# One written list for batch 0 behind its attention: tails, weight pieces, attention blocks and products taken singly

## The chip, the cores and the metric

The kernel runs on one core of a Trainium2 chip. A core has a matrix engine (PE), a vector engine (DVE), a scalar engine (ACT), a general engine (POOL) and SP, which here only issues DMAs. Each engine works through its own instructions in the order in which the program wrote them, and waits at semaphores for the others. The metric is the device time of one execution in microseconds (us), taken as the median over runs. Before the change it was 1199.24 us in three runs (1198.79 to 1200.69).

## The reference

Attention with a sigmoid in the place of the softmax, for 8 batches of 12 heads (448 tokens, 64 dimensions a head), then two dense layers with a gate of their own:

```python
scores = scale * np.matmul(q, k.transpose(0, 1, 3, 2)) - np.log(S)
attn = 1.0 / (1.0 + np.exp(-scores))
attn_out = np.matmul(attn, v).astype(np.float32)
...
h = x @ w_in          # x: 3584 x 768, w_in: 768 x 2048
g = h - np.tanh(h)
return (g @ w_out).astype(np.float32)
```

## The kernel before

**Arithmetic.** fp32 numbers are mostly multiplied as three fp16 products: a high and a low half of each factor, without low times low. The weights come as 64-bit patterns. Each has to be converted to fp32 on the chip (a "piece" is 128 rows of one part of a matrix: load, sign, bits, and a small matmul `wl` that sums magnitudes for a bound), and later split in place into its fp16 halves: `high` on ACT (a few on DVE), `low` on DVE. The slot of a high half is where the fp32 numbers of an earlier row block lay, so a split of one row block waits for those before it.

**Stages of batch 0.** `attention32` computes the attention of batch 0 in fp32 while `w_in` is converted. Then the first dense layer of batch 0 runs in fp32 (`ph` matmuls on unsplit weights, 16 of them in eight pairs, as the hidden units come in 16 groups of 128). After each pair comes its tail (`mix`): ACT makes a square `u` and a tanh `th` from the PSUM tile `ph`, DVE makes `m` and `th` from the same tile, two more squares and products follow, and `halves` writes the fp16 halves `g` of the pair. Only when DVE has read `ph` for `m` and `th` is that PSUM buffer free. Then the second layer (`moe2`) multiplies `g` by the split `w_out`: for batch 0 the left half of the columns first (e = 0: three full token tiles, each of eight products of six matmuls), then the right half (e = 1), then 16 short products for the last 64 tokens.

**What runs beside it.** Batch 0 also has to carry three other streams: the conversion of `w_out` (20 pieces while the first layer runs, 12 more beside the second), the in-place split of `w_out` and `w_in`, and the attention of batch 1 with the first block of batch 2. The attention stream is the generator `stream`. Its first eight steps are preparation (loads, norms, scales, the fp16 halves of K and Q); from step 9 on they are blocks of scores (`sc` on PE), sigmoid (`a` on ACT) and the product with v (`acc` on PE). Each block takes the two PSUM buffers of tag `sc` in turn, and the `ph` pairs use the same two.

**What sets the order.** For the first layer the function `moe1_32` does: after each `ph` group a fixed number of conversion steps (`REST`), at some groups one step of the attention stream (`INIT`), and after each pair its whole tail in one go. The tail of the eighth pair is taken in four portions in `first`, between attention blocks 9 to 13. From then on `second` works off a table of due times (`SPLIT`, `CONV`, `BLOCKS0`, counted in products): after each product everything that is due is written. The order of PE, ACT, DVE and POOL is that of the program there; the DMA issues on SP are placed by the framework. Batches 1 to 7 have tables of their own (`BLOCKS1`, `BLOCKS`).

Of the kernel before, what the change touches and what calls it, by code (L numbers as in the profile page):

```python
# [8 lines left out]
F16 = mybir.dt.float16  # L9
BF16 = mybir.dt.bfloat16  # L10
F32 = mybir.dt.float32
# [22 lines left out]
class Builder:  # L34

    AV32 = 2

    INIT = (0, 4, 6, 7, 8, 10, 12, 14)
    EARLY = 4
    AHEAD = 3  # L40
    LAND = ("o", "o", 2, "v", "v", "v", 1, 0, 3, 4, 5)
    REST = (4, 4) + (2, 1, 1) * 4 + (1, 0)
    SPLIT = tuple(8 + 1.25 * k for k in range(8)) + tuple(22 + 0.85 * k for k in range(36))
    CONV = tuple(3 + 1.2 * k for k in range(1, 6)) + tuple(9 + 0.85 * k for k in range(1, 13))

    BLOCKS = (8, 11, 16, 19, 20, 24, 27, 32, 35, 36, 40, 43, 48, 51, 52)
    TAIL = (1, 2, 3, 4, 5)
    ALONE = 11
    BLOCKS0 = (4, 6, 8, 9, 12, 16, 20, 23, 24, 31, 38)
    BLOCKS1 = (4, 7, 8, 11, 13, 16, 19, 20, 24, 27, 32, 35, 36, 40, 43, 48, 51, 52)  # L50

    TP = 8
# [283 lines left out]
    def norm(self, t, out):  # L336

        flat = t.rearrange("p a d -> p (a d)") if len(t.shape) == 3 else t
        n = flat.shape[1]
        junk = self.sm.tile([P, 8 * D], BF16, name="sqn", tag="sq", bufs=4)  # L340
        self.nc.scalar.activation(junk[:, :n], flat, AF.Square, accum_out=out)  # L341
# [304 lines left out]
    def attention32(self, b, weights, rest):  # L646

        nc = self.nc
        S = self.S
        NP = self.NP  # L650
        xs = []
        tags = (("kn", "qn"), ("K", "Q"))
        self.row = []
        loaded = {}

        def load(j):
            loaded[j] = self.load_qk(b, j, tags[j % 2])
            if j < 2:
                next(weights)
            loaded[j].append(self.load_v(b, j, self.att, "vhl", 3))  # L660

        load(0)
        one = self.sm.tile([P, 1], F32, name="one", tag="m")
        nc.scalar.activation(one, self.nls, AF.Sigmoid)
        next(weights)
        load(1)
        next(weights)
        todo = []
        accs = {}

        def open_acc(j):
            accs[j] = self.ps.tile([P, 512], F32, name="acc", tag="mm", bufs=2)

        def av():
            j, c, a = todo.pop(0)
            v = loaded[j][2][:, None]
            if c == QT:
                open_acc(j + 1)
                self.av([accs[j], accs[j + 1]], v, a, c, 0)
            else:  # L680
                if c == 0 and j % 2 == 0:
                    open_acc(j)
                self.av([accs[j]], v, a, c, j % 2)
            if c == (QT, QT - 1)[j % 2]:
                xs.append(self.evac_x(j, accs.pop(j), None))

        self.warm(12)
        order = [(j, c) for j in range(NP) for c in (range(QT) if j % 2 else range(QT + 1))]
        for n in range(0, len(order), 2):
            group = order[n : n + 2]  # L690
            pss = []
            for j, c in group:
                both = (j, j + 1) if c == QT else (j,)
                K, Q = ([loaded[i][x][:, None] for i in both] for x in range(2))
                pss.append(self.scores(K, Q, c))
            ready = len(todo)
            todo += [(j, c, self.weigh(ps, 1.0 / math.sqrt(D))) for (j, c), ps in zip(group, pss)]
            if n < 4:
                self.warm(4)
            for _ in range(ready):  # L700
                av()
            for j, c in group:
                if c == 1 and j + 2 < NP:
                    load(j + 2)
                next(weights)
                if c == QT:
                    next(weights)
        next(rest)
        while todo:
            av()  # L710
            next(rest)
        next(rest)
        self.xs, self.xs32 = xs, True

    def token_norms(self, nm):
# [65 lines left out]
    def moe1(self, st):  # L781
# [6 lines left out]
        for k in range(self.NF // 2):  # L788
# [19 lines left out]
                pass  # L808
            if k == 0:
                self.Sg, self.iSg = self.g_scales(m)  # L810

    def moe1_32(self, xs, weights, rest):


        nc = self.nc
        S = self.S
        self.gs = []
        self.late = []
        for k in range(self.NF // 2):
            ph = self.ps.tile([P, 2, 512], F32, name="ph", tag="sc", bufs=2)  # L820
            for e in range(2):
                f = 2 * k + e
                for c in range(self.NC):
                    nc.tensor.matmul(  # L824
                        ph[:, e, :S],
                        self.where("in", c)[:, f * P : (f + 1) * P],
                        xs[c],
                        start=(c == 0),
                        stop=(c == self.NC - 1),
                    )  # L830
                if f in self.INIT:
                    next(self.blocks)
                for _ in range(self.REST[f]):
                    next(rest)
                if k == 0 and e == 0:
                    for _ in weights:
                        pass
                    w = self.w_in_scales()
                    m = self.token_norms(self.ps.tile([P, 512], F32, name="nm0", tag="mm", bufs=2))
                elif k < 2:  # L840
                    next(w, None)
                if (k, e) == (1, 1):
                    self.Sg, self.iSg = self.g_scales(m)
                if f == 12:
                    self.w_out_scale(0)
                    self.ahead = self.split_w_out(0)
                if f > 12:
                    next(self.ahead)
                if f == 15:
                    self.w_out_bound(1)  # L850
                    self.split_in = self.split_w_in()
                    next(self.split_in)
            g = self.gp.tile([P, 2, 2, S], F16, name="g", tag="g")
            self.gs.append(g)
            self.tail = self.mix(ph[:, :, :S], g, self.ih0, self.ihk0)
            if k == self.NF // 2 - 1:
                return
            for _ in self.tail:
                pass

    def mix(self, ps, g, ih, ihk):

# [101 lines left out]
    def build(self):  # L964
# [22 lines left out]
        with tc.manual_schedule(engines={E.PE, E.Activation, E.DVE, E.Pool}):  # L987
# [4 lines left out]
                self.attention32(0, weights, rest)  # L992
            self.gp = tc.alloc_tile_pool(name="gp", bufs=self.NF // 2, reuse_waits="tile")
            self.blocks = self.stream()
            self.moe1_32(self.xs, weights, rest)
            assert next(rest, None) is None
            self.first(self.convert(pieces[nB:], "product"))
        with tc.manual_schedule(engines={E.PE, E.Activation, E.DVE, E.Pool, E.SP}):
            for b in range(1, self.B):
                self.batch(b)  # L1000
        self.gp.release()

    def first(self, rest):

        n = 5
        split, ahead = self.split_in, [self.ahead]
        products = self.moe2(0, self.gs)
        next(self.tail)
        for _ in range(self.AHEAD):
            next(products)  # L1010
        next(split)
        for k in range(n - 1):
            if k == 2:
                next(self.blocks)
            next(self.blocks)
            for _ in range(2):
                next(self.tail, None)
            if k == 1:
                next(ahead[0])
            if k == 2:  # L1020
                self.finish_g()
                next(ahead[0])
        next(rest)
        next(ahead[0])
        next(rest)
        assert n + len(self.BLOCKS0) + len(self.BLOCKS1) == 5 * self.NP + len(self.BLOCKS) - self.ALONE
        assert len(self.SPLIT) == self.NC * self.NB - self.SHIFT
        events = [(p, lambda: next(split)) for p in self.SPLIT]
        events += [(k + 0.5, lambda: next(ahead[0], None)) for k in range(self.AHEAD, self.NF // 2 - 3)]
        events += [(p, lambda: next(rest)) for p in self.CONV]  # L1030
        at = math.ceil(self.CONV[-1])

        def scale():
            self.w_out_scale(1)
            ahead[0] = self.split_w_out(1)

        events += [(at, scale)] + [(at + k, lambda: next(ahead[0], None)) for k in range(1, self.NF // 2 + 1)]
        self.second(0, self.BLOCKS0, len(self.BLOCKS0) - 1, events, products, self.AHEAD)

    def batch(self, b):  # L1040

# [16 lines left out]
            blocks = self.BLOCKS1  # L1058
        self.second(b, blocks, alone, events)

    def second(self, b, blocks, alone, events, products=None, done=0):

        step = lambda: next(self.blocks)
        events += [(p, step) for p in blocks]
        scales = []

        def norms():
            scales.append(self.batch_scales(self.xs, b == 0))
            next(scales[0])

        if blocks:
# [2 lines left out]
            events += [(p, lambda: next(scales[0], None)) for p in (end + 5, end + 7)]  # L1074
        events.sort(key=lambda e: e[0])
        full = self.NF * (self.S // P)
        for k, _ in enumerate(products or self.moe2(b, self.gs), done):
            now = k + 1 if k < full else full + (k + 1 - full) / 2
            while events and events[0][0] <= now:
                events.pop(0)[1]()  # L1080
# [35 lines left out]
```

## Time and profile before

| | before |
|---|---|
| median of the runs | 1199.24 us |
| time of the profiled execution | 1198.76 us |
| its span | 1197.0 us |
| PE busy over the span | 1164.3 us (97%) |
| DVE busy over the span | 904.0 us (76%) |
| ACT busy over the span | 884.0 us (74%) |

The span is the time between the first and the last instruction of the profile; the 1.76 us around it belong to the execution. PE is the engine that bounds the whole, so time can be lost or won where PE waits, or where it runs at less than the full clock. The chain of waits puts 71% of the span on PE and nearly nothing on the other engines. How batch 0 stands out against the rest is shown in the prediction.

### The profile page before, as it was taken

To read this page: it belongs to the slowest core of one execution; us is meant where nothing else is said; L and a number is where in the kernel's file an instruction comes from. 1 tells how busy PE (TensorE), PEld (TensorE's weight loads), DVE (VectorE), ACT (ScalarE), POOL (GpSimd) and SP (SyncE) were. 2 spreads that over 40 slices of the span, in tenths; PEclk is the share of its full clock that TensorE was granted. 3 is DMA by queue.
4 is the path that set the end of the run, shared out by engine and by line. 5 is a ranking of instruction groups with operands and counts; after the bars stand their busy time and mean duration, and the time that the engine had idled before them with its cause. 6 is when DMAs were issued, how large, how long until landed. Compare 5 with 4: busy or idle time off the path is not lost.

```text
span 1197.0 us, 19036 instructions
## 1 busy us (share of the span) xinstructions
PE 1164.3 (97%) x7585; PEld 602.9 (50%) x7585; DVE 904.0 (76%) x1335; ACT 884.0 (74%) x1248; POOL 76.3 (6%) x58
## 2 busy tenths in 40 slices
PE   9999779999999999999999999999999999999998
PEld 2344324455545555555555555555555555555555
DVE  6889868769866897778966798578977699646920
ACT  7878688868988588767788588876887688745820
POOL 0000000000021000200012000110012000200000
PEclk9999899999999999999999999999999999999999
DMA  9941043200122100220022100211012200000000
GB/s 364 344 146 55 16 133 123 67 14 1 39 68 74 38 1 30 82 60 16 1 69 67 52 1 16 74 60 39 1 49 72 67 1 2 29 27 8 1 14 33
DMA packets 34057, 70.43 MB, mean 59 GB/s; under 512 B 3888, under 2 KB 21040, under 8 KB 33968
## 3 DMA queue, kind: packets, MB, share of 16 engines
q1 hardware_dynamic: 33824, 68.99, 17.6%
q8 instruction: 59, 0.97, 0.3%
q14 instruction: 30, 0.25, 0.1%
q10 hardware_dynamic: 144, 0.23, 0.1%
HBM read 58.20 MB, written 11.01 MB: 58 GB/s over the span
## 4 chain that ended last, share of the span: by engine, by line
PE 71%; ACT 1%; DVE 0%; issue 0%; ACTq 0%; DVEq 0%
PE ph L794 27%; PE po L912 27%; PE sc L399 6%; PE acc L430 6%; PE por L950 5%; ACT a L410 0%; DVE ahl L417 0%; PE pbn L349 0%; ACT ahl L416 0%; ACT o L941 0%; PE nm L718 0%; ACT sqn L341 0%; ACT x L444 0%; ACT Q L374 0%; DVE orem L959 0%
## 5 line engine op out<-in xcount | busy, mean ns | idle before, releaser
L912 PE MATMUL po<-wo,g 128*128 128x384 f16 x2304 | 396.8, 327 | 10.1 <-ACT wo L226 4.9
L794 PE MATMUL ph<-xhl,wi 128*128 128x448 f16 x2016 | 382.6, 352 | 0.0
L912 PEld LDWEIGHTS <-g 128*128 128x128 f16 x2304 | 220.2, 98 | 181.1 <-issue 42.9
L794 PEld LDWEIGHTS <-wi 128*128 128x128 f16 x2016 | 196.7, 98 | 185.0 <-issue 2.1
L417 DVE SCALAR_TENSOR_TENSOR ahl<-a,ahl 128x896 f16<-128x896 f32 x126 | 160.8, 1311 | 134.4 <-ACT ahl L416 134.3
L410 ACT ACTIVATE a<-sc,nls,rn 128x896 f32<-128x896 f32 x147 | 156.0, 1091 | 49.1 <-PE sc L399 48.9
L867 ACT ACTIVATE u<-ph,ih 128x896 f32<-128x896 f32 x64 | 64.4, 1006 | 83.8 <-PE ph L794 81.9
L416 ACT ACTIVATE ahl<-a 128x896 f16<-128x896 f32 x126 | 113.2, 941 | 0.6
L399 PE MATMUL sc<-Q,K 64*128 64x448 f16 x1008 | 102.9, 358 | 7.1 <-ACT a L410 6.1
L871 DVE SCALAR_TENSOR_TENSOR m<-ph,ihk,u 128x896 f32<-128x896 f32 x64 | 73.4, 1146 | 37.3 <-ACT th L869 37.0
L778 ACT ACTIVATE g<-m,Sg 128x896 f16<-128x896 f32 x64 | 66.6, 1041 | 33.6 <-DVE m L885 26.2
L885 DVE COPY_PREDICATED m<-u,th 128x896 f32<-128x896 uint32 x64 | 77.3, 1208 | 6.6
L430 PE MATMUL acc<-ahl,vhl 128*64 128x448 f16 (+1 forms) x864 | 80.6, 356 | 0.1
L779 DVE SCALAR_TENSOR_TENSOR g<-m,Sg,g 128x896 f16<-128x896 f32 x64 | 73.2, 1144 | 7.7 <-ACT g L778 7.7
L882 DVE SCALAR_TENSOR_TENSOR m<-q,m 128x896 f32<-128x896 f32 x64 | 69.9, 1092 | 10.2 <-ACT q L881 2.8
L461 POOL TENSOR_TENSOR x<-x 128x448 f32<-128x448 f32 x24 | 26.4, 1098 | 773.2 <-ACT x L444 773.2
L824 PE MATMUL ph<-x,wi 128*128 128x448 f32 x192 | 75.1, 541 | 0.0
L872 DVE SCALAR_TENSOR_TENSOR th<-ph,ih,th 128x896 f32<-128x896 f32 x64 | 73.1, 1143 | 0.0
L884 ACT ACTIVATE u<-u,b 128x896 f32<-128x896 f32 x64 | 66.7, 1043 | 4.0 <-DVE m L871 2.0
L399 PEld LDWEIGHTS <-K 64*128 64x128 f16 x1008 | 36.5, 98 | 65.8 <-issue 41.4
L878 DVE SCALAR_TENSOR_TENSOR m<-q,m 128x896 f32<-128x896 f32 x64 | 69.4, 1084 | 0.0
L950 PE MATMUL por<-wo,g 128*64 128x384 f16 x768 | 65.8, 327 | 1.1 <-ACT o L941 1.1
(139 smaller groups left out, 1144.1 us busy)
## 6 DMA issues: line engine op xcount, KB each, us to landing
knn<-k SPq DMA_DIRECT2D x45, 224.0 KB, 2.6
qnn<-q SPq DMA_DIRECT2D x44, 224.0 KB, 2.6
rawo<-moe_w_out SPq DMA_DIRECT2D x22, 384.0 KB, 5.2
out<-o SPq DMA_DIRECT2D x21, 384.0 KB, 2.3
raw<-moe_w_in SPq DMA_DIRECT2D x13, 512.0 KB, 8.0
vn<-v SPq DMA_DIRECT2D x24, 256.0 KB, 2.9
wo<-moe_w_in SPq DMA_DIRECT2D x11, 512.0 KB, 8.1
vn<-v SPq DMA_DIRECT2D x24, 192.0 KB, 2.4
```

The lines of the kernel that those rows point to most:

```text
L399: self.nc.tensor.matmul(ps[i * m : (i + 1) * m, h, : self.S], K[i][r, w, c * P : c * P + m], Q[i][r, x, :], start=(n == 0), stop=(n == len ...
L410: self.nc.scalar.activation(a[:, 0], ps[:, :, : self.S], AF.Sigmoid, bias=self.nls, scale=scale)
L416: nc.scalar.activation(A[:, 0], a[:, 0], AF.Copy, scale=A_SCALE)
L417: nc.vector.scalar_tensor_tensor(A[:, 1], a[:, 0], A_SCALE, A[:, 0], op0=ALU.mult, op1=ALU.subtract)
L430: self.nc.tensor.matmul(acc[i][h * D : (h + 1) * D, : self.S], v[k, w, 2 * QT + h if half else h * QT + c], A[k, x, h], start=(n == 0 and ...
L779: nc.vector.scalar_tensor_tensor(g[:, 1], m, Sg, g[:, 0], op0=ALU.mult, op1=ALU.subtract)
L794: nc.tensor.matmul(ph[:, e, :S], self.wi[:, c * self.NB + k, part, e * P : (e + 1) * P], xhl[c][:, x, :], start=(i == 0), stop=(i == 3 * s ...
L824: nc.tensor.matmul(ph[:, e, :S], self.where("in", c)[:, f * P : (f + 1) * P], xs[c], start=(c == 0), stop=(c == self.NC - 1),)
L871: V.scalar_tensor_tensor(m, ps, ihk, u, op0=ALU.mult, op1=ALU.mult)
L885: V.copy_predicated(m, u.bitcast(U32), th)
L912: nc.tensor.matmul(po[i][:, :H], gs[f // 2][:, x, f % 2, tk * P : (tk + 1) * P], self.wo[:, i * self.NF + f, w], start=(f == 0 and n == 0) ...
L950: nc.tensor.matmul(po[e * D : (e + 1) * D, :H], gs[f // 2][:, x, f % 2, nm:S], self.wo[:, e * self.NF + f, w], start=(f == 0 and n == 0), ...
```

## The change

The functions `moe1_32`, the tables `INIT`, `REST`, `SPLIT`, `CONV`, `BLOCKS0` and the events of batch 0 go. In their place stands one string of 272 letters; the new `first` walks it and does one step for each letter:

- M one `ph` group (six chunks of fp32 matmul); t one of the six steps of a pair's tail (the first makes `u`, `th`, `m`, `th`; the second the `g` halves of the pair before; the sixth does nothing on an engine); F the `g` halves that are still due
- R one conversion step beside the first layer, C one beside the second, W the rest of the attention's conversion
- n, w, g, N the bounds and scales (token norms, `w_in`, `g`, and the scales of batch 1's input); x, b, X the scale or bound of `w_out`
- A the split of two row blocks of `w_out`, S one step of the split of `w_in`
- B one step of the attention stream, P one product of the second layer

Below and in the prediction a letter with a number is the n-th of its kind: B9 is the first block with scores, B12 the step that scales the heads of the second pair, P8 the last product of the first token tile (it needs the `g` of the eighth pair), A4 the fourth split. The step `t43` is the first of the eighth pair's tail, the one that frees its PSUM buffer.

```diff
-    INIT = (0, 4, 6, 7, 8, 10, 12, 14)
-    AHEAD = 3
-    REST = (4, 4) + (2, 1, 1) * 4 + (1, 0)
-    SPLIT = tuple(8 + 1.25 * k for k in range(8)) + tuple(22 + 0.85 * k for k in range(36))
-    CONV = tuple(3 + 1.2 * k for k in range(1, 6)) + tuple(9 + 0.85 * k for k in range(1, 13))
-    BLOCKS0 = (4, 6, 8, 9, 12, 16, 20, 23, 24, 31, 38)
+    ORDER = (
+        "RRRMRRRnRRWRMRBRwRtRttRRtttMBwMRwgttRMtRBtttMtttBtRttMMRtttRtRttMBMtRtxtR"
...
+        "SBSSPPPSSSPSSNPPSSPPPSPSPNPSNSPPSSPSPSPPPPSSPPPPSSPPPPSS"
+    )
...
+    def first(self, weights, early, late):
...
+        steps = {
+            "M": mixture,
...
+            "R": lambda: next(early),
...
+            "t": lambda: next(self.tail, None),
+            "F": self.finish_g,
+            "P": lambda: next(products),
+            "B": lambda: next(self.blocks),
+            "A": lambda: next(self.ahead),
+            "C": lambda: next(late),
...
+            "S": lambda: next(split),
+            "N": norm,
+        }
+        for step in self.ORDER:
+            steps[step]()
```

The number of steps of each kind is the same, and so are the instructions; one of the conversion steps that stood at the end of `attention32` is now the first letter. Batches 1 to 7 keep their tables. What moves is shown at three places.

The first is DVE at the last `ph` pair. In the kernel before, these rows stand around the step that frees the pair's PSUM buffer (`m` and `th` from `ph`; `wo<-wo,swo_s` is a low half of `w_out`, `wi` one of `w_in`, `g` a low half of the gate):

```order
L228 TENSOR_SCALAR wo<-wo,swo_s 128x384
L231 SCALAR_TENSOR_TENSOR wo<-wo,swo_s 128x384 x2
L291 TENSOR_REDUCE mo<-wl 128x1
L871 SCALAR_TENSOR_TENSOR m<-ph,ihk_110,u 128x896
L872 SCALAR_TENSOR_TENSOR th<-ph,ih_108,th 128x896
L898 TENSOR_SCALAR iK<-iswo,iSg 128x1
L231 SCALAR_TENSOR_TENSOR wi<-wi,swi_s 128x256 x4
L779 SCALAR_TENSOR_TENSOR g<-m,Sg,g 128x896
```

In the changed kernel the same place of DVE reads:

```order
L835 COPY_PREDICATED m<-u,th 128x896
L231 SCALAR_TENSOR_TENSOR wo<-wo,swo_s 128x384 x2
L291 TENSOR_REDUCE mo<-wl 128x1
L821 SCALAR_TENSOR_TENSOR m<-ph,ihk_110,u 128x896
L822 SCALAR_TENSOR_TENSOR th<-ph,ih_108,th 128x896
L778 SCALAR_TENSOR_TENSOR g<-m,Sg,g 128x896
L228 TENSOR_SCALAR wo<-wo,swo_s 128x384
L231 SCALAR_TENSOR_TENSOR wo<-wo,swo_s 128x384 x2
```

The split ahead of the step is now A4 and no longer A3 (A3 stands before the tail steps of the pair before), and the first four low halves of `w_in` have gone from the second row behind the step to the twentieth.

The second is PE around the small matmul `pbn` in B12, from which the scales of the next two heads come (`po` a product of the second layer, `acc` the product with v, `sc` scores). Before:

```order
L399 MATMUL sc<-Q,K 128x448
L430 MATMUL acc<-a_1159,vn 64x448 x2
L430 MATMUL acc<-a_1161,vn 64x448 x4
L349 MATMUL pbn<-ss_116,onesf 128x4
L399 LDWEIGHTS K
L399 MATMUL sc<-Q,K 128x448
```

And in the changed kernel, where the six matmuls of a product end ahead of `pbn`:

```order
L862 LDWEIGHTS g
L862 MATMUL po<-wo,g 128x384
L349 MATMUL pbn<-ss_116,onesf 128x4
L862 LDWEIGHTS g
L862 MATMUL po<-wo,g 128x384
L862 LDWEIGHTS g
L862 MATMUL po<-wo,g 128x384
```

A product now stands before `pbn` and another behind it, where the blocks followed each other directly; six products have moved from behind B14 to places between the blocks 9 to 14.

The third is DVE behind that matmul, as far as the `g` of the eighth pair. Before, the scale chain of five small instructions was followed by the K and Q halves and at once by that `g`:

```order
L362 SCALAR_TENSOR_TENSOR rn<-in 128x1
L376 TENSOR_SCALAR K<-knn,sn 128x448
L377 SCALAR_TENSOR_TENSOR K<-knn,sn,K 128x448
L377 SCALAR_TENSOR_TENSOR Q<-qnn,sn,Q 128x448
L779 SCALAR_TENSOR_TENSOR g<-m,Sg,g 128x896
```

Now two more splits stand between:

```order
L362 SCALAR_TENSOR_TENSOR rn<-in 128x1
L376 TENSOR_SCALAR K<-knn,sn 128x448
L377 SCALAR_TENSOR_TENSOR K<-knn,sn,K 128x448
L377 SCALAR_TENSOR_TENSOR Q<-qnn,sn,Q 128x448
L231 SCALAR_TENSOR_TENSOR wo<-wo,swo_s 128x384 x2
L231 SCALAR_TENSOR_TENSOR wi<-wi,swi_s 128x256 x4
L778 SCALAR_TENSOR_TENSOR g<-m,Sg,g 128x896
```

The `g` that P8 needs has A8 and the first four low halves of `w_in` in front of it, while P8 itself has come forward to directly behind B13.

More of the change, by code (lines that the diff above doesn't have):

```diff
@@ L36 @@
     AV32 = 2
-    INIT = (0, 4, 6, 7, 8, 10, 12, 14)
     EARLY = 4
-    AHEAD = 3
     LAND = ("o", "o", 2, "v", "v", "v", 1, 0, 3, 4, 5)
-    REST = (4, 4) + (2, 1, 1) * 4 + (1, 0)
-    SPLIT = tuple(8 + 1.25 * k for k in range(8)) + tuple(22 + 0.85 * k for k in range(36))
-    CONV = tuple(3 + 1.2 * k for k in range(1, 6)) + tuple(9 + 0.85 * k for k in range(1, 13))
+    ORDER = (
+        "RRRMRRRnRRWRMRBRwtRttRRtttMBwMRwgttRMtRBtttMtttBtRttMMRtttRtRttMBMtRtxtR"
+        "RtttMMBtttARtAtMtRMBtttABtttMMAbttAPttPBPAtBACtPPBPBASPSFBPCCCPPBPPCSCPC"
+        "SBPCBBCPCSSPSCCSPSBCCBCPCCSPCPCBXAPAPAPAPBPSPABAAPPPASSSBSPPPSPSSSPPSSPS"
+        "SBSSPPPSSSPSSNPPSSPPPSPSPNPSNSPPSSPSPSPPPPSSPPPPSSPPPPSS"
+    )
     BLOCKS = (8, 11, 16, 19, 20, 24, 27, 32, 35, 36, 40, 43, 48, 51, 52)
@@ L711, in attention32 @@
             next(rest)
-        next(rest)
         self.xs, self.xs32 = xs, True
@@ L810, in moe1 @@
                 self.Sg, self.iSg = self.g_scales(m)
[L812 to L859, printed above, removed]
     def mix(self, ps, g, ih, ihk):
@@ L994, in build @@
             self.blocks = self.stream()
-            self.moe1_32(self.xs, weights, rest)
-            assert next(rest, None) is None
-            self.first(self.convert(pieces[nB:], "product"))
+            self.first(weights, rest, self.convert(pieces[nB:], "product"))
         with tc.manual_schedule(engines={E.PE, E.Activation, E.DVE, E.Pool, E.SP}):
@@ L1001, in build @@
         self.gp.release()
-    def first(self, rest):
-        n = 5
-        split, ahead = self.split_in, [self.ahead]
-        products = self.moe2(0, self.gs)
[L1008 to L1038, printed above, removed]
@@ new lines, in first, with mixture, drain, token_bound @@
+    def first(self, weights, early, late):
+        nc = self.nc
+        S = self.S
+        xs = self.xs
+        self.gs, self.late = [], []
+        split = self.split_w_in()
+        bound = self.w_in_scales()
+        products = self.moe2(0, self.gs)
+        norms, phs = [], []
+        def mixture():
+            e = len(phs)
+            if e == 0:
+                phs.append(self.ps.tile([P, 2, 512], F32, name="ph", tag="sc", bufs=2))
+            ph = phs[0]
+            f = 2 * len(self.gs) + e
+            for c in range(self.NC):
+                nc.tensor.matmul(
+                    ph[:, e, :S],
+                    self.where("in", c)[:, f * P : (f + 1) * P],
+                    xs[c],
+                    start=(c == 0),
+                    stop=(c == self.NC - 1),
+                )
+            if e:
+                g = self.gp.tile([P, 2, 2, S], F16, name="g", tag="g")
+                self.gs.append(g)
+                self.tail = self.mix(ph[:, :, :S], g, self.ih0, self.ihk0)
+                phs.clear()
+        def drain():
+            for _ in weights:
+                pass
+        def token_bound():
+            self.m0 = self.token_norms(self.ps.tile([P, 512], F32, name="nm0", tag="mm", bufs=2))
+        def g_bound():
+            self.Sg, self.iSg = self.g_scales(self.m0)
+        def scale(e):
+            self.w_out_scale(e)
+            self.ahead = self.split_w_out(e)
+        def norm():
+            if not norms:
+                norms.append(self.batch_scales(self.xs, True))
+            next(norms[0], None)
+        steps = {
+            "M": mixture,
+            "W": drain,
+            "n": token_bound,
+            "w": lambda: next(bound, None),
+            "g": g_bound,
+            "R": lambda: next(early),
+            "x": lambda: scale(0),
+            "b": lambda: self.w_out_bound(1),
+            "t": lambda: next(self.tail, None),
[4 more added lines that the diff above has]
+            "C": lambda: next(late),
+            "X": lambda: scale(1),
+            "S": lambda: next(split),
[3 more added lines that the diff above has]
+            steps[step]()
+        for gen in (products, split, early, late, norms[0]):
+            assert next(gen, None) is None
@@ L1059, in batch, with second @@
         self.second(b, blocks, alone, events)
-    def second(self, b, blocks, alone, events, products=None, done=0):
+    def second(self, b, blocks, alone, events):
         step = lambda: next(self.blocks)
@@ L1067, in norms @@
         def norms():
-            scales.append(self.batch_scales(self.xs, b == 0))
+            scales.append(self.batch_scales(self.xs, False))
             next(scales[0])
@@ L1076, in second @@
         full = self.NF * (self.S // P)
-        for k, _ in enumerate(products or self.moe2(b, self.gs), done):
+        for k, _ in enumerate(self.moe2(b, self.gs)):
             now = k + 1 if k < full else full + (k + 1 - full) / 2
```

## The prediction

> **What bounds the kernel now.** I read the page's slices first. The row PE is the busy share of PE in 40 slices of 29.9 us, in tenths; PEclk is the clock that PE was granted.
>
> ```profile
> span 1197.0 us, 19036 instructions
> PE   9999779999999999999999999999999999999998
> PEclk9999899999999999999999999999999999999999
> ```
>
> PE is full everywhere but in the fifth and sixth slices, about 120 to 180 us, and only there does the clock fall. Next the view of stretches from the first `ph` matmul (52.9) to the first matmul of batch 1 (250.5): length, busy time of PE, weight loads, DVE and ACT, then the clock.
>
> ```profile
> 52.90:132.50 79.60, 78.97 (x232) 39.40 (x231) 69.75 (x115) 60.49 (x95) 0.00 (x0) 1.00 0.31 101
> 132.50:180.00 47.50, 31.91 (x193) 12.46 (x191) 34.98 (x64) 40.79 (x70) 1.14 (x1) 0.89 0.28 87
> 180.00:230.00 50.00, 45.47 (x300) 22.21 (x296) 43.40 (x98) 44.17 (x91) 3.49 (x3) 1.00 0.35 106
> 52.90:250.50 197.60, 176.85 (x887) 86.17 (x885) 162.18 (x307) 162.16 (x288) 4.62 (x4) 0.97 0.29 91
> ```
>
> Batch 0 behind its attention lasts 197.6 us, in which PE works 176.85: 20.75 us idle, 15.6 of them between 132.5 and 180. The slow clock adds to this. Two stretches hold nearly all of it:
>
> ```profile
> 137.50:144.00 6.50, 5.13 (x18) 1.97 (x18) 4.80 (x9) 4.53 (x9) 0.00 (x0) 0.51 0.00 0
> 167.50:172.50 5.00, 4.38 (x28) 1.65 (x27) 2.36 (x6) 4.97 (x9) 1.14 (x1) 0.66 0.58 201
> ```
>
> At clocks of 0.51 and 0.66, busy times of 5.13 and 4.38 lose 2.5 and 1.5 us against the full clock. So the most an order can win is 20.75 + 4.0 = 24.7 us. DVE and ACT have 162 us of work each, so they fit into a shorter stage only if they hardly wait. The view of waits says for what PE waits (total, times, longest):
>
> ```profile
> PE sc L399 <- ACT a L410: 6.1, 7, 2.2
> PE po L912 <- ACT wo L226: 4.9, 2, 4.0
> PE po L912 <- DVE wo L231: 3.2, 5, 1.3
> PE pbn L349 <- ACT sqn L341: 2.0, 1, 2.0
> ```
>
> **The change part by part.** Nothing is added or removed; the sum is made of waits. I cut the stage at two points that both kernels share: the second score unit of B9, and the end of B14's scores.
>
> *Up to B9.* PE in order of time (start, duration, work, count, idle before):
>
> ```profile
> 132.46 1.14 PE L912 MATMUL po<-wo,g 128*128 128x384 f16 x6
> 137.58 0.48 PE L912 MATMUL po<-wo,g 128*128 128x384 f16 x1 [3.97 <-ACT wo L226]
> 139.35 3.67 PE L912 MATMUL po<-wo,g 128*128 128x384 f16 x11 [1.30 <-DVE wo L231]
> 142.96 1.30 PE L399 MATMUL sc<-Q,K 64*128 64x448 f16 x6
> 145.45 1.31 PE L399 MATMUL sc<-Q,K 64*128 64x448 f16 x12 [1.19 <-ACT a L410]
> ```
>
> P2 waits for its split. That split (A2) now stands before M13, over 15 us earlier, so both waits of P2 go. But what is late next is the buffer: B9's second unit needs the PSUM buffer of the eighth pair, which DVE frees with `th`, and PE will stand there instead.
>
> ```profile
> 140.19 1.15 DVE L231 SCALAR_TENSOR_TENSOR wo<-wo,swo_s 128x384 f16<-128x384 f32 x2
> ...
> 144.43 1.14 DVE L872 SCALAR_TENSOR_TENSOR th<-ph,ih,th 128x896 f32<-128x896 f32 x1
> ```
>
> DVE ends this at 145.57, when the second unit starts (145.45; ends on PE are modelled). Up to there DVE has the same work in the new order plus A4's low halves, 1.15. What can shrink are its own waits on the way:
>
> ```profile
> DVE m L871 <- ACT th L869: 5.4, 5, 1.6
> DVE m L720 <- PE nm L718: 2.0, 1, 2.0
> DVE stb L172 <- ACT rawo L166: 0.8, 1, 0.8
> DVE st L274 <- PE cn L272: 0.5, 1, 0.5
> ...
> 66.81 1.15 DVE L871 SCALAR_TENSOR_TENSOR m<-ph,ihk,u 128x896 f32<-128x896 f32 x1 [1.41 <-ACT th L869]
> ```
>
> Together 8.7. The first wait on `th` was 1.41; the other four (4.0) go, since with pieces and splits spread between the tail steps DVE reaches a tail about 2 us after ACT has made it ready. Of the early 4.7, the token norms (n) now stand between conversion steps that are already loaded, and I let 1.8 go. So `th` ends at 145.57 + 1.15 - 4.0 - 1.8 = 141.0; with nothing saved 146.7, with all of it 138.0. PE still ends the `ph` work at 132.5, does P1, P2 and the first unit by 135, and waits 6 us.
>
> *From there to B14.* A product costs 0.99 (42 matmuls between the next two starts make 6.92); a score unit 0.65 (half of a row of 12), the product of two units with v 1.72:
>
> ```profile
> 235.70 6.99 PE L912 MATMUL po<-wo,g 128*128 128x384 f16 x42
> 242.62 7.99 PE L950 MATMUL por<-wo,g 128*64 128x384 f16 x96
> ...
> 148.07 1.72 PE L430 MATMUL acc<-a,vn 128*64 128x448 f32 x8
> 162.44 0.74 PE L399 MATMUL sc<-Q,K 64*128 64x448 f16 x6 [0.71 <-ACT a L410]
> ```
>
> From 141.0: the second unit 0.65, P3, P4, P5, P6 (4.0), B10 and B11 (each 1.3 and 1.7) give `pbn` at 151.7. Behind `pbn` stands the chain on DVE that ends in the `g` for P8:
>
> ```profile
> 158.50 0.16 DVE L355 TENSOR_TENSOR un<-tn 128x2 f32<-128x2 f32 x1 [1.83 <-ACT tn L351]
> ...
> 159.36 0.45 DVE L376 TENSOR_SCALAR K<-knn,sn 128x448 f16<-128x448 f32 x1
> ...
> 161.04 1.14 DVE L779 SCALAR_TENSOR_TENSOR g<-m,Sg,g 128x896 f16<-128x896 f32 x1
> ```
>
> ACT's `tn` 0.25, the five small instructions 0.86 (158.50 to 159.36), K and Q halves 1.68 (to 161.04), A8 1.15, the four `wi` low halves 1.66 and `g` 1.14:
>
> ```profile
> 145.61 1.66 DVE L231 SCALAR_TENSOR_TENSOR wi<-wi,swi_s 128x256 f16<-128x256 f32 x4
> ...
> L351 ACT ACTIVATE tn<-pbn,tiny 128x4 f32<-128x4 f32 x3 | 0.8, 253 | 0.0
> L931 ACT ACTIVATE oh<-po,iK 128x384 f32<-128x384 f32 x6 | 3.4, 568 | 0.6 <-issue 0.6
> L226 ACT ACTIVATE wi<-wi,swi_s 128x256 f16<-128x256 f32 x48 | 21.5, 495 | 0.0
> ```
>
> That is 6.7, so `g` is there at 158.4. PE has P7 and B13 (3.4) behind `pbn` and reaches P8 at 155.3: a new wait of 3.1 us. P8, P9, P10 and B14's scores (4.3) end at 162.7. For the slow clock after two waits I add 1.5: 164.2. Before, the same point lay at 162.44 + 0.74 = 163.2, with four products done instead of ten. Six products are 5.9, less 1.0: **4.9 won**. If P8 need not wait 8.0; if `th` comes at 146.7, 5.7 less, so -0.8.
>
> *From B14 to batch 1.* Before:
>
> ```profile
> 163.10:250.50 87.40, 79.00 (x544) 39.58 (x542) 69.60 (x158) 75.26 (x153) 4.62 (x4) 0.98 0.34 106
> ```
>
> 8.4 us idle, and the 1.5 us of the second slow stretch. The `wo` waits there (P5, P6, and three of the right half) go, as A8 is done before P8 and the right half's A9 to A16 stand singly from P20 on, with A12 four products before it is used. The wait of B16's `pbn` for ACT's norms (2.0, row above) stays: only P14 stands between. P17 follows the eviction of P16 with two conversion matmuls between, which I price at 0.5 (an `oh` takes ACT 0.57, row above). I leave 1.5 for small waits and 0.5 for the clock. So 8.4 + 1.5 - 4.5 = **5.4 won**; bounds 0 (each gap returns elsewhere) and 9.9. The last S steps now run to the end of the list. They cost PE nothing, as P49 to P64 cover their 0.5 us each on ACT (row above) and as much on DVE, and batch 1's first groups use row blocks split earlier.
>
> The sum: 4.9 + 5.4 = 10.3. Against the profiled execution, whose span of 1197.0 and 1.76 around it make 1198.76, this gives 1188.5; against the median, 1199.24, about 1189.
>
> [...] After an idle time of 3.97 us the clock stood at 0.51 for 6.5 us. [...] The second slow stretch, at 167.5, has no gap over 1 us near it, so the rows decide for some cost. [...]
>
> **The rivals.**
> - *The waits hide better* (0.15). If DVE never waits up to `th` (138.0, 3.0 earlier) and C wins 8 of its 9.9, the gain is 16 to 18: 1182. For it: DVE and ACT have 162 us in what would be 180.
> - *DVE only moves the wait* (0.18). PE meets DVE at three new places (B9, P8, B16). If `th` comes at 144, 3 later, and half of the last part returns, the gain is 10.3 - 3.0 - 2.7 = 4.6: 1194.6.
> - *Loads in line, slower* (0.08). C2, C3, C4 stand together behind P8, so the piece loaded at C2 is signed at C4 with no PE work between, and ACT holds B14's sigmoids behind it. The loads stand on SP behind K and Q of a head whose buffer B12 frees at about 154. Rows of before:
>
> ```profile
> 165.78 10.05 SPq L149 DMA_DIRECT2D rawo<-moe_w_out  x4
> ...
> rawo<-moe_w_out SPq DMA_DIRECT2D x12, 384.0 KB, 4.2
> ```
>
>   Four took 10 us to issue and 4.2 each to land. Landed one after another they come at 158, 162, 167, and ACT would wait some 3 us at each of four to five pieces: 13 us, and 1199.2 - 10.3 + 13 = 1202. It decides from 10 us of such waits on; if the loads are issued as early as their buffers come free, after B10 at about 146 by the sum above, there are none.
> - *The clock swings* (0.06). Short groups between short waits could hold the clock at 0.66, as at 167.5. Over the 40 us of PE work from 141 to 190 that loses a third, 13 us: about 1202. Against it stands this row, 7.7 us idle in many short gaps at a clock of 0.99:
>
> ```profile
> 144.00:167.50 23.50, 15.79 (x108) 5.95 (x105) 16.79 (x31) 20.03 (x32) 0.00 (x0) 0.99 0.27 84
> ```
>
> - *No change* (0.05): both halves of the gain come back as waits, 1198. That the order does not do what it says I leave out, since the rows of the order show the steps moved.
>
> **How the numbers follow.** Forecast 0.48 at 1189; the rivals as given. The range reaches to the better case and over most of the moved-wait case, whose bound (a gain of 1 to 2) I take in: 1180 to 1197. About 0.2%, 2.4 us, is what a measurement of this kernel can tell from no change. Faster: 0.48 + 0.15 + 0.18 and a little of the slower ones' better ends, 0.83; same 0.08; slower 0.09.
>
> **What would show it.** Right: PE's wait before P2 gone, one of 5 to 7 us inside B9, one of 2 to 4 before P8, about 12 to 15 us idle in the stage, batch 1 starting near 240. Wrong: `th` of the eighth pair later than 144, ACT waiting for `rawo`, or a clock under 0.9 over 150 to 190.

## The result and the profile after

The changed kernel takes 1185.88 us in the median of four runs (1184.65 to 1187.38), beside 1199.01 us for the kernel before on the same chip: a ratio of 0.9889 with a 95% interval of 0.9872 to 0.9906, or 13.1 us less. The forecast was 1189, the range 1180 to 1197. The profiled execution is the fastest of the four, 1184.65 us, and 14.1 us under the profiled one of before; the forecast of 10.3 stands against this 14.1.

First the same slices as before, from the page of the changed kernel:

```profile
span 1182.8 us, 19017 instructions
PE   9999889999999999999999999999999999999998
PEclk9999999999999999999999999999999999999999
```

PE's hole in the fifth and sixth slices is down to two eights, and no slice of 30 us shows a low clock (a shorter slow stretch is left; the rows stand in the last section). The view of stretches (length, then busy time of PE, weight loads, DVE, ACT and POOL, the clock, DMA) for the stage from the first `ph` matmul to batch 1, and for its troubled part:

```profile
52.59:236.40 183.81, 172.84 (x887) 84.89 (x886) 158.49 (x303) 160.81 (x286) 4.68 (x4) 0.99 0.30 98
132.50:180.00 47.50, 39.13 (x259) 16.26 (x259) 36.63 (x73) 40.81 (x71) 2.28 (x2) 0.96 0.44 143
```

The stage is 183.8 us long instead of 197.6. PE is idle in 11.0 of them instead of 20.75, and its busy time is 4.0 less for the same 887 matmuls. So 13.8 us of the 14.1 were won in this stage; the rest of the kernel takes what it took (1182.8 - 183.8 = 999.0, before 999.4).

The waits of PE in the stage (total, times, longest):

```profile
PE sc L399 <- DVE th L822: 3.4, 1, 3.4
PE po L862 <- ACT g L777: 2.1, 1, 2.1
PE sc L399 <- ACT a L410: 1.6, 1, 1.6
PE pbn L349 <- ACT sqn L341: 1.4, 1, 1.4
PE po L862 <- DVE g L778: 0.8, 1, 0.8
PE po L862 <- ACT oh L881: 0.7, 1, 0.7
```

The waits of products for their splits, 8.1 us before, are gone but for 0.4. In their place stand the two new waits of the forecast, in B9 for `th` and in P8 for `g`. PE in order of time shows both:

```profile
131.62 2.11 PE L862 MATMUL po<-wo,g 128*128 128x384 f16 x12
...
137.76 0.74 PE L399 MATMUL sc<-Q,K 64*128 64x448 f16 x6 [3.36 <-DVE th L822]
...
148.63 0.28 PE L349 MATMUL pbn<-ss,onesf 128*128 128x4 f32 x2
...
154.31 0.50 PE L862 MATMUL po<-wo,g 128*128 128x384 f16 x2 [2.08 <-ACT g L777]
155.64 4.45 PE L862 MATMUL po<-wo,g 128*128 128x384 f16 x16 [0.82 <-DVE g L778]
160.02 1.31 PE L399 MATMUL sc<-Q,K 64*128 64x448 f16 x12
...
169.28 0.39 PE L349 MATMUL pbn<-ss,onesf 128*128 128x4 f32 x2 [1.40 <-ACT sqn L341]
```

P1 and P2 run through without a wait. B9's second unit starts at 137.76, P8 waits 2.1 and 0.8, and B14's scores end at 160.02 + 1.31 = 161.33. On DVE the two releasers of these waits:

```profile
136.56 1.14 DVE L822 SCALAR_TENSOR_TENSOR th<-ph,ih,th 128x896 f32<-128x896 f32 x1
...
154.43 1.15 DVE L778 SCALAR_TENSOR_TENSOR g<-m,Sg,g 128x896 f16<-128x896 f32 x1
```

`th` of the eighth pair ends at 137.70, before it was 145.57. That is 3.3 us earlier than forecast, and the largest miss of the sum.

### The profile page after: what moved, and what is told of

Its sections match the earlier page's. It is cut to its first block, busy times and chain, and to the rows that moved or that the text cites. A ratio compares the mean times of both kernels' runs of the same rounds, so it can differ in the third digit from the quotient of the medians.

```text
span 1182.8 us, 19017 instructions
## 1 busy us (share of the span) xinstructions
PE 1160.8 (98%) x7585; PEld 601.6 (51%) x7585; DVE 902.2 (76%) x1335; ACT 883.8 (75%) x1248; POOL 76.4 (6%) x58
## 4 chain that ended last, share of the span: by engine, by line
PE 72%; ACT 1%; DVE 0%; issue 0%; ACTq 0%; DVEq 0%
PE ph L793 28%; PE po L862 27%; PE sc L399 6%; PE acc L430 6%; PE por L900 5%; ACT a L410 0%; DVE ahl L417 0%; PE pbn L349 0%; ACT ahl L416 0%; ACT o L891 0%; PE nm L717 0%; ACT sqn L341 0%; ACT x L444 0%; ACT Q L374 0%; DVE orem L909 0%
```

## The experiments

All are other orders of the same steps: only the string of letters differs, and nothing is left out (back_old has three letters t more, which find their tail at its end and do nothing). Of the string only the parts that differ are shown. Runs that are compared closely shared a chip and the runs of the kernel before on it: 1199.12 us for front_old, back_old, grouped and f_early; 1199.10 for control, s_late, s_late_f and s_late_f_p; 1198.92 for the three that begin with c_later; 1199.56 for the last.

### Which half of the list wins (front_old, back_old)

front_old writes the steps up to M16 and the split A3 behind it in the order of before, back_old those behind M16, the eighth pair's tail included:

```diff
front_old
-RRRMRRRnRRWRMRBRwtRttRRtttMBwMRwgttRMtRBtttM
+RMBRRRRWnMRRRRwttttttMRRwMRwgttttttMBRMRRttt
...
-RtttMMBtttARtAtMtRMBtttABtttMMAbttAPtt
+RRttttttMBRxMRAttttttMBRAMAAbttAPtt
back_old
-MMAbttAPttPBPAtBACtPPBPBASPSFBPCCCPPBPPCSCPCSBPC
+MMbStPPPSBttBttABBttFABttCACPABPCAPCBPCPCSBPCBPS
...
```

> Old order of steps up to the last ph group and A3, the new list from A4 on. Theory: the gain of 13.1 us has a front half (DVE frees the eighth pair's PSUM buffer at 137.7 and not at 145.6) and a back half (products as cover, splits and conversions spread). Then the second score unit of B9 starts near 145.2, P2 waits again for its split (about 5 us), and the time is about 1193.5 (7.5 over the changed kernel). Rival A, the back half does it all: 1186 to 1187. Rival B, the front half does it all: 1198 to 1199.

> The new list up to the last ph group, the old order behind it. Theory: the buffer comes free near 137, B9's second unit follows there, P2 does not wait, and what is lost is the back half: about 1191.5. Rival A, the back half does it all: 1198 to 1199, since DVE's old order behind B9 makes PE wait wherever it stands. Rival B, the front half does it all: 1186 to 1187.

front_old took 1193.84 us (0.9954, 0.9939 to 0.9969), back_old 1190.41 (0.9923, 0.9908 to 0.9938). The back half alone thus wins 5.3 us and the front half alone 8.7; together 14.0, where the change wins 13.1. The two are nearly independent. What the early split A2 and the early `th` win within the front half these two runs do not separate. From PE's timeline of front_old:

```profile
137.14 0.32 PE L862 MATMUL po<-wo,g 128*128 128x384 f16 x1 [3.97 <-ACT wo L226]
138.91 1.76 PE L862 MATMUL po<-wo,g 128*128 128x384 f16 x5 [1.45 <-DVE wo L231]
145.12 1.30 PE L399 MATMUL sc<-Q,K 64*128 64x448 f16 x6 [3.21 <-DVE th L822]
```

With the old front, P2's two waits are back, one to the hundredth (3.97) and one nearly so (1.45, before 1.30), and the buffer for B9 comes at 145.1 as before. In back_old the opposite holds:

```profile
136.97 1.31 PE L399 MATMUL sc<-Q,K 64*128 64x448 f16 x12 [1.54 <-DVE th L822]
...
147.86 1.30 PE L399 MATMUL sc<-Q,K 64*128 64x448 f16 x6 [2.25 <-ACT a L410]
```

The buffer comes as early as in the changed kernel (136.97, there 137.76), but the blocks follow each other directly, and PE waits for sigmoids again.

### What brought `th` forward (grouped)

In the first seven tails the third, fourth and fifth steps, which work on the same tile `m`, are written directly behind each other. What stood between them (pieces, blocks, `ph` groups) moves in front of or behind the three.

```diff
-RRRMRRRnRRWRMRBRwtRttRRtttMBwMRwgttRMtRBtttMtttBtRttMM
+RRRMRRRnRRWRMRBRwtRttttRRtMBwMRwgttRMtttRBtMtttttBRtMM
...
```

> The new list, but the third, fourth and fifth step of each of the first seven tails stand directly behind each other; what stood between (10 places with work for DVE) follows the fifth. Theory: on DVE a step that uses what the step right before it wrote starts 1.19 us after it, and 1.00 with another instruction between, so DVE is through the eighth pair's buffer 10 x 0.19 = 1.9 us later (139.6 for 137.7), PE waits that much longer inside B9, and the time is 1187 to 1188. Rival, the spacing is no more than a moved idle time and DVE has slack there: no change, 1185.9, and the buffer free at 137.7.

1189.03 us (0.9912, 0.9897 to 0.9927), about 3 more than the changed kernel and 1 to 2 more than expected. `th` ends at 141.19, 3.5 later, and B9 waits 5.24. DVE in order of time, first in the kernel before, then in the changed kernel, then in this run:

```profile
81.43 1.08 DVE L878 SCALAR_TENSOR_TENSOR m<-q,m 128x896 f32<-128x896 f32 x1
82.63 1.09 DVE L882 SCALAR_TENSOR_TENSOR m<-q,m 128x896 f32<-128x896 f32 x1
```

```profile
99.99 1.08 DVE L828 SCALAR_TENSOR_TENSOR m<-q,m 128x896 f32<-128x896 f32 x1
100.99 0.57 DVE L172 SCALAR_TENSOR_TENSOR stb<-stb,rawo 128x384 uint32<-128x384 uint32 x1
```

```profile
100.52 1.08 DVE L828 SCALAR_TENSOR_TENSOR m<-q,m 128x896 f32<-128x896 f32 x1
101.71 1.09 DVE L832 SCALAR_TENSOR_TENSOR m<-q,m 128x896 f32<-128x896 f32 x1
```

The same instruction, 1.08 us long by its row, is followed after 1.00 us by one that works on another tile, and after 1.19 or 1.20 us by one that uses the `m` just written. In the opened pairs the next one is a smaller instruction, but its size is not what matters: `m` and `th` of the eighth pair, 1.14 us each, both 128x896 and independent of each other, start at 135.50 and 136.56, which is also 0.08 less than the duration. In the seven tails up to that `th` there were 14 such pairs; the changed list opens ten of them, 1.9 us. grouped closes them again. Most of the rest of its 3.5 us is waiting. The waits of DVE from the stage's start to that `th`, first of the changed kernel, then the one row of grouped that differs:

```profile
DVE stb L172 <- ACT rawo L166: 0.8, 1, 0.8
DVE m L821 <- ACT th L819: 0.8, 1, 0.8
DVE m L719 <- PE nm L717: 0.5, 1, 0.5
DVE st L274 <- PE cn L272: 0.3, 1, 0.3
```

```profile
DVE m L821 <- ACT th L819: 2.3, 4, 0.9
```

1.9 and the 1.5 more of waits make 3.4. So the expected spacing was there, and the waits on `th` were what the expectation left out: the interleaving of the tails is worth about 3 us, in two ways at once.

### Can the new wait before P8 be taken away (f_early, control, s_late, s_late_f)

f_early takes the `g` for P8 (F) from behind A8 and the `wi` low halves to directly behind the last tail step; s_late strikes the first four letters S and puts four more near the end. So all S steps come later: S1 (four high halves of `w_in` on ACT) and S2 (their low halves on DVE), which stood ahead of that `g`, now stand where S5 and S6 stood, behind C10. s_late_f does both. control is the changed kernel again.

```diff
f_early
-PBPAtBACtPPBPBASPSFBPCCC
+PBPAtBACtFPPBPBASPSBPCCC
s_late
-BPBASPSFBPCCCPPBPPCSCPCSBPCBB
+BPBAPFBPCCCPPBPPCCPCBPCBB
...
-SPSPPPPSSPPPPSSPPPPSS
+SPSSPPPPSSSPPPPSSSPPPPSSS
```

> The new list with F (the g halves of the eighth pair) right behind the last tail step, ahead of P4, where DVE stands idle 3.0 us before the scale chain of B12. Theory: P8 no longer waits (2.1 and 0.8 us), the clock stays full behind it (1.4 us), 1182 to 1183. Rival, the same wait comes back at the next meeting of PE and ACT (pbn of B16, scores of B19): the wait before P8 is gone and the time is the same, 1185.9.

> The changed kernel itself, as the measure for the three beside it on the same chip. All theories: 1185 to 1187, with 11 us of PE idle in the stage.

> The new list without its first four S letters (the ones between A8 and B15); four more S stand among the last products, so the first four low halves of w_in are split behind B17. Theory: the term of 1.66 us in the chain from pbn to the g of P8 goes (and 1.69 on ACT ahead of that g), the waits before P8 fall from 2.9 to about 1.2, and the slow stretch behind them goes as well: 1.7 to 3 us less than the control. Rival, the middle of the stage is bound by ACT as a whole and the wait moves on to pbn of B16: same as the control.

> As s_late, and F right behind the last tail step as in f_early. Theory: no wait before P8 at all and ACT free for the sigmoids and norms of B14 and B15 (its 1.7 us gone), so the wait of pbn in B16 stays near 1.4 to 2 where f_early had 4.2: 2.5 to 4 us less than the control. Rival, what held ACT in f_early was the piece that landed late (1.7 us), and pbn waits 3 to 4 us again: within 1 us of the control.

| | us | ratio to before, 95% interval |
|---|---|---|
| control | 1186.12 | 0.9892 (0.9874 to 0.9909) |
| f_early | 1187.36 | 0.9898 (0.9881 to 0.9914) |
| s_late | 1187.12 | 0.9895 (0.988 to 0.9911) |
| s_late_f | 1185.69 | 0.9891 (0.9873 to 0.9909) |

None is measurably better, as the rivals had it, though in f_early and s_late_f no wait is left before P8, and in s_late only 1.3 us. This row of f_early shows where the 2.9 us went; the same wait was 1.40 in the changed kernel and 2.7 and 3.2 in the other two:

```profile
171.76 0.39 PE L349 MATMUL pbn<-ss,onesf 128*128 128x4 f32 x2 [4.17 <-ACT sqn L341]
```

PE is not the engine that is late at B16: `pbn` needs ACT's norms, and these do not come earlier because PE does.

### What holds ACT (s_late_f_p, c_later, c_later_p, c_later_p_t43)

s_late_f_p takes P3 and P4 in front of B9, to fill its wait. The three others build on it: c_later has the pieces C5 to C7 behind B15 (c_later_p also three products in front of B16's `pbn`), and c_later_p_t43 has the step t43 ahead of A4 and the bound b, with P4 behind B9 again.

```diff
s_late_f_p, on s_late_f
-AbttAPttPBPAtBACtFPPBPBA
+AbttAPttPPPBAtBACtFPBPBA
c_later, on s_late_f_p
-BPPCCPCBPCBBCPC
+BPPPBCCPBCCBCPC
c_later_p, on s_late_f_p
-BPPCCPCBPCBBCPC
+BPBCPPPCBCCBCPC
c_later_p_t43, on c_later_p
-MMAbttAPttPPPBAt
+MMtAbtAPttPPBPAt
```

> As s_late_f, and P3 and P4 ahead of B9, so that PE fills two of the 3.4 us in which it waits there for the buffer of the eighth pair. Theory: the wait inside B9 falls to about 1.4, but B10 to B12 stand against ACT (sigmoids, splits and norms without a pause from 137 to 145), so at most 0.5 to 1 us of it is kept. Rival, the products are worth their full 2 us, since nothing behind B9 is bound by ACT.

> The order of s_late_f_p, but the pieces C5 to C7 are signed behind the block B15 instead of ahead of it. Theory (ACT, in order, stands 2.2 us at a piece whose load lands late, and so holds B15's sigmoids and the norms that pbn of B16 waits for): no wait of ACT for rawo ahead of B15's sigmoids, the wait of pbn falls from 3.7 to about 1.5 us, about 2 us less than s_late_f_p: 1182.5. Rival (the loads only come as late and the wait stands at the next use, wl or the sigmoids of B17; or pbn waits for something other than the pieces): within 0.7 us of s_late_f_p, 1184 to 1185.

> As c_later, and the products P12, P13 and P14 stand between B15 and B16, ahead of the small matmul pbn. Theory: three products, 3 us, cover what is left of the chain over ACT's norms, the wait of pbn is below 0.5 us, 3 to 3.5 us less than s_late_f_p: 1181 to 1181.5. Rival (the time is set by ACT's and DVE's work and not by where PE waits): the wait goes to the sigmoids of B15 or to wl, no more than 1 us less than s_late_f_p, 1183.5 to 1184.5.

> As c_later_p, and the step t43, which frees the PSUM buffer of B9's second unit, stands ahead of the split A4 and of the bound b, with P4 back behind B9. Theory: th ends about 1.6 us earlier (A4's two low halves and the bound are behind it), the wait inside B9 stays near 1 us or below with one product less in front of it, and P4 fills PE later: 0 to 1.4 us less than c_later_p. Rival (th waits for ACT, which makes u and th of the pair, so DVE gains a wait in the place of A4): th ends at the same time, B9 waits about 2.4 us, 0.5 to 1 us more than c_later_p.

s_late_f_p took 1184.52 us (0.9877, 0.9862 to 0.9893). B9 now waits 1.4 instead of 3.4, and the time is 1.2 us less than that of s_late_f, between what the theory (0.5 to 1) and the rival (2) expected. Of the 2.0 us taken from B9, 1.4 come back before P8, where PE now waits for the two halves of the split A8 (0.56 and 0.86). The next row is PE's `pbn` of B16, then the row of ACT that explains it:

```profile
167.03 0.39 PE L349 MATMUL pbn<-ss,onesf 128*128 128x4 f32 x2 [3.68 <-ACT sqn L341]
```

```profile
163.32 0.57 ACT L164 ACTIVATE stb<-rawo 128x384 f32<-128x384 f32 x1 [2.19 <-DMA rawo<-moe_w_out]
163.78 2.09 ACT L410 ACTIVATE a<-sc,nls,rn 128x896 f32<-128x896 f32 x2
```

ACT stands 2.19 us at a piece whose load has not landed, and B15's sigmoids and the norms stand behind it. c_later puts these pieces behind the block: 1182.99 us (0.9867, 0.9851 to 0.9884), 1.5 less in the median and 1.2 by the two ratios, where 2 were expected. The wait of `pbn` falls to 1.73. The theory expected no wait for a load ahead of B15's sigmoids, and there it was wrong: the wait of 2.19 is gone, but ACT now stands 2.02 at the piece ahead of B14's sigmoids (0.42 in s_late_f_p), whose load landed about 1.6 us later. In all, ACT's waits for `rawo` between 140 and 200 fell only from 2.6 to 2.2. Part of the gain is given back at P17, where the eviction `oh` stands on ACT behind four high halves of `w_in`. PE and then ACT in c_later:

```profile
164.97 0.39 PE L349 MATMUL pbn<-ss,onesf 128*128 128x4 f32 x2 [1.73 <-ACT sqn L341]
...
176.87 1.14 PE L862 MATMUL po<-wo,g 128*128 128x384 f16 x6 [2.39 <-ACT oh L881]
```

```profile
158.26 0.55 ACT L164 ACTIVATE stb<-rawo 128x384 f32<-128x384 f32 x1 [2.02 <-DMA rawo<-moe_w_out]
...
174.66 1.69 ACT L226 ACTIVATE wi<-wi,swi_s 128x256 f16<-128x256 f32 x4
176.26 0.56 ACT L881 ACTIVATE oh<-po,iK 128x384 f32<-128x384 f32 x1
```

c_later_p took 1183.81 (0.9873, 0.9858 to 0.9888; single runs from 1181.48 to 1185.79). Its `pbn` waits 0.34 as forecast, but `oh` 3.04: another 1.4 us less here, 0.65 more there, and no difference in the time that these runs can tell. Its profiled execution is the fastest of its four, so these rows show it at its best. c_later_p_t43 took 1183.66 (0.9872, 0.9857 to 0.9887):

```profile
136.13 0.74 PE L399 MATMUL sc<-Q,K 64*128 64x448 f16 x6 [0.90 <-DVE th L822]
...
140.15 0.74 PE L399 MATMUL sc<-Q,K 64*128 64x448 f16 x6 [2.20 <-ACT a L410]
```

`th` ends at 136.07, 1.4 us earlier than in c_later_p, and the wait in B9 falls to 0.9 with one product less to cover it. Theory and rival both missed what follows: the next unit waits 2.2 us for the sigmoids instead, and the time stays.

### The eviction behind the high halves (s_behind_p17)

On top of c_later, the five S steps that stand between C10 and B18 (where the changed kernel's list has S5 to S9) go behind P17 and B18:

```diff
-CPCSSPSCCSPSBCCBCPC
+CPCPCCPBSSCSCSBSCPC
```

> The order of c_later, but the five steps S5 to S9 stand behind the product P17 and the block B18 instead of in front of them. Theory (the wait of 2.4 us before P17 is the eviction oh, which ACT takes only after four high halves of w_in, 1.69 us): oh comes 1.7 us earlier, P17 waits 0.5 to 0.9 us, 1.5 to 1.7 us less than c_later: 1181.4. Rival (ACT's work is only moved: the four high halves then hold the sigmoids of B19 or the next eviction): the wait before P17 falls, but one of 1 to 2 us appears at B18 or B19, and the time stays within 0.7 us of c_later, 1182.3 to 1183.7.

1188.07 us (0.9904, 0.9888 to 0.9921): 5 us more than c_later in the median and 4.4 by the two ratios, worse than theory and rival. The wait for `oh` did fall to 1.45, but the wait that came in its place is larger. PE, then ACT:

```profile
179.20 0.74 PE L399 MATMUL sc<-Q,K 64*128 64x448 f16 x6 [2.56 <-ACT a L410]
...
190.67 0.48 PE L193 MATMUL wl<-stb,onesb 128*128 128x384 bf16 x1 [2.96 <-DVE stb L175]
```

```profile
177.60 0.55 ACT L164 ACTIVATE stb<-rawo 128x384 f32<-128x384 f32 x1 [3.39 <-DMA rawo<-moe_w_out]
178.06 1.08 ACT L410 ACTIVATE a<-sc,nls,rn 128x896 f32<-128x896 f32 x1
```

The high halves had been the work under which the loads landed (in c_later the wait for `rawo` at this place is 0.16, and ACT can sign the piece at 178.05 there and at 177.60 here). Without them ACT comes to the piece early and stands there 3.39 us, with the next sigmoids behind it. The high halves come afterwards all the same, and now DVE waits for one of them, with the bits of a piece behind it that `wl` needs:

```profile
189.26 0.48 DVE L231 SCALAR_TENSOR_TENSOR wi<-wi,swi_s 128x256 f16<-128x256 f32 x1 [2.07 <-ACT wi L226]
```

So ACT's work was only moved, as the rival said, but its price was not 0 to 0.7 us. The clock adds to it, by the view of stretches of this run:

```profile
180.00:185.00 5.00, 5.00 (x19) 1.78 (x20) 4.14 (x10) 5.00 (x14) 0.00 (x0) 0.68 0.31 92
...
190.00:195.00 5.00, 4.33 (x24) 1.40 (x24) 3.14 (x13) 2.37 (x3) 0.00 (x0) 0.51 0.00 0
```

In c_later the clock is 1.00 in both. At 0.68 and 0.51, busy times of 5.00 and 4.33 lose 1.6 and 2.1 us. But c_later has a slow stretch of its own earlier (0.66 from 165 to 170, 0.89 from 165 to 180, where this run has 0.99), which loses 1.7. And two of this order's executions have the mean clock of c_later, 0.998, and still take 1187.65 and 1187.70 us. So the waits make the larger part of the loss.

## Why the forecast was right, and where its sizes were off

- **What is late next** was named rightly at both places: B9's buffer and the `g` for P8 are the two largest waits that are left, and batch 1 starts at 236.4, forecast near 240. Two of its own signs lie outside: the stage is idle for 11.0 us, not 12 to 15, and B9 waits 3.4, not 5 to 7.
- **`th` at 141.0 was mis-sized; it measured 137.70**, just past the bound of 138.0. DVE's waits up to it fell from 8.7 to 2.4, by 6.3 where 5.8 was forecast, and the stage began 0.3 earlier. The step that failed is "DVE has the same work in the new order": the instructions are the same, but the time they take depends on what stands next to what. The ten opened pairs are the 1.9 us that no row of waits could show, and grouped confirms them. Some 0.6 us I cannot place.
- **The wait in B9**, forecast at 6, measured 3.4 for that reason: 137.70 against 141.0.
- **The wait before P8**, forecast at 3.1, measured 2.08 + 0.82 = 2.9. The chain on DVE was sized well; PE and DVE both came 3 us earlier. What the prediction did not name is that the first 2.08 are a wait for the high half of `g` from ACT, which stands behind four high halves of `w_in` there (1.69) and ends at 154.26; the low half on DVE ends at 155.58.
- **Up to B14's scores** 4.9 was forecast, and 163.2 - 161.33 + 5.9 = 7.8 measured; the difference of 2.9 is `th`'s 3.3 passed on, less some tenths.
- **From B14 to batch 1** 5.4 was forecast, and 250.5 - 236.4 - 7.8 = 6.3 measured. B16's `pbn` waits 1.4 instead of 2.0, P17 0.7 instead of 0.5, and the small waits are 2.1 instead of 1.5 (1.65 of it at scores for a sigmoid): 4.2 idle where 4.0 was forecast. The clock costs nothing there instead of 0.5. The other 0.6 lie in PE's busy time.
- **The slow clock after the two waits**, carried at 1.5 as an estimate, cost about 1.6 in this execution, all of it behind P8 and none behind the longer wait in B9 (the rows stand in the last section). That the size fits is luck: in control, the same kernel, both waits were followed by a slow stretch, and together they cost about 4.
- Of PE's busy time that fell by 4.0, the clock explains 2.4, as 1.6 of the 4.0 from before are still lost. What the other 1.6 were, with the 0.6 above among them, I have not traced.

**The rivals.** Of "the waits hide better" the `th` at 138.0 came true as a number and not for its reason: DVE still waits 2.4 us on the way, and the 1.9 of spacing made up for most of it. The other half (8 won behind B14) did not come; the time lies between this case and the forecast. "DVE only moves the wait" did not occur: `th` did not come at 144. Its idea holds for what is left, on another engine: what f_early took away came back at B16, and part of what c_later_p took away at P17, both times as a wait for ACT. "Loads in line" did not occur either: ACT waits 1.4 us for `rawo` between 140 and 200 in the changed kernel. Waits of its kind occur, however: ACT waits 2.6 us for `rawo` in s_late_f_p, and 4.7 in s_behind_p17, which lost about 5 us against c_later. "The clock swings" did not occur: the clock is 0.96 from 132.5 to 180.

The best order found, c_later, takes 1182.99 us, about 3 less than the changed kernel. That is two steps, measured one after the other at 1.2 and 1.5 us: two products cover part of B9's wait, and later pieces take ACT's wait for a load away from in front of B15. Its single runs (1182.49 to 1183.42) all lie below those of the changed kernel (1184.65 to 1187.38), while the intervals of the two ratios still overlap a little. Whether s_late and f_early are needed for it was not tried.

## What to carry to other kernels

Where an engine that works in order is spread over several streams, a wait removed on the bounding engine is only worth what the next chain leaves: follow it to the engine that releases the next wait, and move that engine's work. Work in front of an instruction that waits for a load is cover for the load (ACT waited 0.16 us for a piece behind the high halves in c_later, and 3.39 without them in s_behind_p17), so ask before moving it what it was covering. And of two orders with the same instructions, the one that puts another stream between dependent instructions can be faster even if no wait is shown: on DVE here 1.00 us from start to start instead of 1.19, ten times.

## What the runs showed of the hardware

**Dependent neighbours on DVE.** In the seven tails up to the eighth pair's `th`, the distance from the start of a step that writes `m<-q,m` (128x896, fp32) to the next start is 1.19 or 1.20 us in all 14 pairs of the kernel before, where the next one uses the result. In the changed kernel it is 1.18 or 1.19 in the four pairs left and 1.00 or 1.01 in the ten opened, where the next one works on another tile: about 0.11 more or 0.08 less than the duration of 1.08. That the neighbour's size is not the cause shows in the pair of `m` and `th` named in grouped's section (1.06 apart, 1.14 long). The durations of the profile's rows, 1.07 to 1.09 in either case, don't tell the two apart.

**The clock after a wait differs between executions.** The view of stretches, in the changed kernel and in control, which is the same kernel:

```profile
137.70:142.00 4.30, 4.24 (x36) 1.67 (x38) 4.15 (x8) 4.28 (x6) 0.00 (x0) 1.00 0.00 0
154.30:157.00 2.70, 1.86 (x9) 0.92 (x10) 2.66 (x5) 2.70 (x7) 0.00 (x0) 0.89 0.93 308
157.00:160.00 3.00, 3.00 (x11) 1.22 (x8) 2.30 (x6) 1.26 (x3) 0.00 (x0) 0.53 0.70 241
```

```profile
137.70:142.00 4.30, 4.29 (x18) 1.31 (x18) 4.15 (x7) 3.72 (x5) 0.00 (x0) 0.50 0.00 0
...
157.00:162.00 5.00, 4.50 (x20) 1.93 (x20) 3.96 (x7) 3.83 (x9) 0.00 (x0) 0.68 0.77 264
```

After the same wait in B9 (3.36 and 3.38 us) the clock was full in one execution and 0.50 in the other; after the two gaps of 2.1 and 0.5 to 0.8 before P8 it was low in both. Cut finer, the view has 0.50 from 156.40 to 159.80 in the changed kernel; in control it still has 0.89 from 142 to 147, behind the first of its two stretches. What decides between the two outcomes of one wait these runs do not show.

Single shorter waits show the same: after 2.24 us in the kernel before (B13's scores at 156.33) the clock stayed at 1.00 until 160, after 1.73 in c_later (164.97) it was 0.66 from 165 to 170, and after 2.25 in back_old (147.86) six score matmuls took 1.30 us, where six take 0.74 at 152.83 of that run. So here a wait of 1.73 to 3.38 us came with a slow stretch or without one: in the changed kernel and in control each stretch cost 1.4 to 2.7 us of matmul time by the clocks above. Slow stretches may also be part of why runs of one order differ: the four of the changed kernel go from 1184.65 us at a mean clock of 0.998 to 1187.38 at 0.995, those of s_late from 1184.80 at 0.999 to 1187.91 at 0.995; the four of c_later_p do not follow it (1184.67 at 0.996, 1185.79 at 0.997).
